# A spectral-mixing and gated-convolution kernel: one table load at the head, batch 1's folds one a step, exponents behind copies

## The chip, the cores and the metric

One Trainium2 chip; the program runs on 1 of its cores. A core has TensorE (PE, matrix products into PSUM), VectorE (DVE), ScalarE (ACT), GpSimd (POOL) and SyncE (SP, which here only starts DMAs). Each engine works through its own list of instructions in order and waits for the others by semaphores. The metric is the device time of one execution in microseconds; lower is better. Of the kernel before there are 3 runs.

## The reference

The input x has 8 batches of 3136 rows and 256 columns. The first half is the real part of a two-dimensional Fourier transform, the second a gated convolution:

```python
X = np.fft.fft(x, axis=1)
x = np.fft.fft(X, axis=2).real.astype(np.float32)
h = np.maximum(x @ w_in, 0.0)                 # 256 -> 1024
for k in range(3):                            # hp: h padded by one row on each side
    conv_out += conv_w[k] * hp[:, k:k + S, :]
gate = 1.0 / (1.0 + np.exp(-conv_out))
out = (h * gate) @ w_out                      # 1024 -> 256
```

The weights come as 64-bit floats and are narrowed to 32 bits on the chip.

## The kernel before

The transform along the rows is done as products with small tables of cosines and sines, after the input has been *folded*: rows that share a cosine or a sine up to sign are added and subtracted first. The transform along the columns is multiplied into w_in once, which gives G. So batch b needs a fold (`fold_ops`, VectorE), eight *units* of products against the tables (`units`, PE, each with a copy on ScalarE and an ending `fin` on VectorE), which give the tiles pt and qt, and then the main loop.

**The main loop** has 256 steps, one for each batch (8), chunk of rows (4) and group of 128 hidden columns (8): 32 steps a batch (`per`). Step t issues, engine by engine, work for several stages at once. On PE: `products` of step t+1 (pb from qt, then pa from pt; pb has one buffer, pa two), then `mm2` of step t-5, the block po<-wout,g of six tiles and 12 matmul records. On ScalarE: the sigmoid of step t-4 (L826), then whatever is put down under "first", `copies` of step t+1 (pb into nb, L788), what is put down under "act", the `seed` of step t+2 (L767, which writes pa before PE adds to it), the first tap (L802); and, where a chunk ends (steps 12, 20, 28 and so on), the copies of the output (L859) ahead of its stores. On VectorE: `combine` of step t (L796), what is put down under "dve", the last tap of step t-3 (L811), the gate of step t-4 (L835). On GpSimd: its share of the gate (L834), in a batch's first chunk the clearing of two columns of the next h (`row_of`, L773), the middle tap as an adding DMA (L806), what is put down under "pool", and the gathers under "load". The output of the gate of one step is the left operand of PE's block in the next.

**What is put down where** is written out in the program: a table `side` with a step and a place for each piece (`at`). The pieces that matter here:
- `shared`: in steps 0, 2, 4, 6, 8 and 10 a part of a weight is narrowed. Its first part, `power`, stands under "first": a shift on VectorE (L619) and the exponent on ScalarE (L621, a Relu activation). The second, `product`, under "dve": L633, L634, L627, L637. L627 needs the exponent.
- `Feature`: a small transform for one column; tables on ScalarE in steps 11 to 13 (L520 to L533), two products on PE in steps 14 and 16 with VectorE's L544 in step 15, and the same again in steps 31 to 34.
- The folds of batch b stand in the steps of a list `cs`, 16 operations, eight for each half of the rows: 0 pair(0) (L157), 1 pair(2) (L157, L160), 2 both(6) (L168), 3 feats(1) (L194, L195), 4 both(4) (L168), 5 turned (L228), 6 evens (L172, L173), 7 feats(0) (L194, L195), and 8 to 15 the same for the second half. `turned` multiplies by a factor and adds a copy scaled on ScalarE, `scaled` (rt<-w, L222), which for b over 0 stands under "act" in the step of operation 5 (and 13), the same step as `turned`. `scaled` reads what feats(1) and GpSimd's `single(1)` (L179, L181) write.
- For batch 1 `cs` is written out. For the others the steps go evenly from `ends[b-1]` to `ends[b]`, past steps already taken. In the step after a half's last operation the load of xh for the next batch begins: one DMA on SP, then four gathers on GpSimd (L132), one a step (for the second half three small DMAs on SP come between). Batch 2's folds stand in steps 23 to 42, with the gathers of batch 3's first half in steps 35 to 38.
- The units of batch b stand from `ends[b]` on (batch 1: two steps before it), under "pe" behind the block; copy and ending come in the step after the last part. For batch 1: one unit a step in steps 21 to 28, endings in 22 to 29. psd, the bank they use, has one buffer. Batch 1's tiles pt and qt are first read by the products issued in step 31.

ScalarE loads its function table where a function first needs one that is not in it: at the head before the copy of the taps (L698), and once more before the first sigmoid, in step 4.

Of the kernel before, what the change touches and what calls it, by code (L numbers as in the profile page):

```python
# [9 lines left out]
F32 = mybir.dt.float32  # L10
I32 = mybir.dt.int32
U32 = mybir.dt.uint32
AF = mybir.ActivationFunctionType
# [24 lines left out]
def kernel(  # L38
# [11 lines left out]
    B, S, D = x.shape  # L50
    F = moe_w_in.shape[1]
    P = 128
# [16 lines left out]
    const = ctx.enter_context(tc.tile_pool(name="const", bufs=1))  # L69
# [20 lines left out]
    act = nc.scalar.activation  # L90
# [51 lines left out]
    def fold_ops(b):  # L142

        def half(h):
            k = slice(0, NP if h == 0 else KR)
            qs = slice(2 * h, 2 * h + 2)

            def t():
                return xh[b, h]

            def pair(m):
                def f():
                    a, r = t()[k, m:m + 2], t()[k, 7 - m:5 - m:-1, ::-1, :]
                    vt(a[:, :, :, 1:D], a[:, :, :, 1:D], r[:, :, :, D - 1:0:-1], op=ALU.add)  # L157
                    if m == 2:
                        a, r = t()[k, 0:4], t()[k, 7:3:-1, ::-1, :]
                        vt(a[:, :, :, 0], a[:, :, :, 0], r[:, :, :, 0], op=ALU.add)  # L160
                return f

            def flat(i, j):
                return t()[k, i:j].rearrange("p s q d -> p (s q d)")

            def both(to, op):
                def f():
                    vt(flat(to, to + 2), flat(0, 2), flat(2, 4), op=op)  # L168
                return f

            def evens():
                vt(flat(0, 1), flat(4, 5), flat(5, 6), op=ALU.add)  # L172
                vt(flat(1, 2), flat(4, 5), flat(5, 6), op=ALU.subtract)  # L173

            def single(odd):

                def f():
                    w, s = wt[b][odd], 6 * odd
                    nc.gpsimd.tensor_copy(w[k, 0:2, qs, 0], t()[k, s:s + 2, :, 0])  # L179
                    if b:  # L180
                        nc.gpsimd.memset(w[k, 2:4, qs, P - 1:P], 0.0)  # L181
                return f

            def feats(odd):
                def f():
                    if h == 0 and odd:
                        wt[b] = [wp.tile([P, 4, HQ, P], F32, name="w", tag="w%d" % i) for i in range(2)]
                        if b == 0:
                            ea[b] = ep.tile([P, 2, HQ], F32, name="ea", tag="ea")
                            nc.gpsimd.memset(wt[b][0][0:KR, 2:4, :, P - 1:P], 0.0)  # L190
                    w, s = wt[b][odd], 6 * odd
                    v = t()[k, s:s + 2]
                    lo, hi = v[:, :, :, 1:P], v[:, :, :, D - 1:P:-1]
                    vt(w[k, 0:2, qs, 1:P], lo, hi, op=ALU.add)  # L194
                    vt(w[k, 2:4, qs, 0:P - 1], lo, hi, op=ALU.subtract)  # L195
                    if b:
                        return
                    single(odd)()
                    if odd:
                        gt(w[k, 2:4, qs, P - 1], t()[k, 7:5:-1, :, P], sg[k], op=ALU.mult)  # L200
                    else:
                        nc.gpsimd.tensor_copy(ea[b][k, :, qs], v[:, :, :, P])
                return f

            def sides():
                w = wt[b][1][0:NP, :, 2 * h]
                return w[:, 0:4:2], w[:, 1:4:2]

            made = []

            def scaled():
                if b == 0:
                    a, c = sides()
                    for i, (v, k) in enumerate(((a, 0), (c, 2), (a, 1), (c, 0))):
                        if i % 2 == 0:
                            parted[h, i // 2] = hp.tile([P, HW], F32, name="h", tag="h")[:, 0:4 * P].rearrange(
                                "p (a s d) -> p a s d", a=2, s=2)
                        act(parted[h, i // 2][0:NP, i % 2], v, AF.Copy, scale=turn[0:NP, k, h:h + 1])
                    return
                made.append(rp.tile([P, 2, 2, P], F32, name="rt", tag="rt"))  # L220
                for i, v in enumerate(sides()):
                    act(made[0][0:NP, i], v, AF.Copy, scale=turn[0:NP, 1, h:h + 1])  # L222

            def turned():
                if b == 0:
                    return
                for i, v in enumerate(sides()):
                    stt(out=v, in0=v, scalar=turn[0:NP, 0, h:h + 1], in1=made[0][0:NP, 1 - i],  # L228
                        op0=ALU.mult, op1=ALU.add if i else ALU.subtract)

            ops = [pair(0), pair(2), both(6, ALU.subtract), feats(1), both(4, ALU.add), turned, evens, feats(0)]
            return ops, {3: single(1), 7: single(0)}, {5: scaled}

        parts = [half(h) for h in range(2)]
        n = len(parts[0][0])
        return (parts[0][0] + parts[1][0],
                *[{n * h + j: f for h in range(2) for j, f in parts[h][i].items()} for i in (1, 2)])
# [363 lines left out]

    low = const.tile([P, 1], F32, name="low")
    nc.gpsimd.memset(low, -896.0 * 2 ** 23)

    def narrow(dst, raw, room=None):

# [106 lines left out]
    for f in load_ops(0, 1, nc.sync, nc.scalar, True):  # L713
        f()

    w_cv.narrow(0, 1)
    w_in[0].narrow(0, 2)
    taps()
# [192 lines left out]
    n = chunks[0].k1  # L911
# [31 lines left out]

    ends = [9, 23, per + 12] + [per * (b - 1) - 3 + max(11 - 4 * (b - 2), 0) for b in range(3, B)]
    def free(cycle):

        while cycle in taken:
            cycle += 1  # L950
        taken.add(cycle)
        return cycle
# [12 lines left out]

    for b in range(1, B):
        begin, us, *_ = units(b)
        us = us[0:4] + us[5:]

        c0 = ends[b] - 2 * (b == 1)  # L970
        n = per * b - 3 - c0
        at(max(c0, per * (b - 1) + 1), "pe", begin)
        cs = [c0 + i * n // len(us) for i in range(len(us) + 1)]
        for i, u in enumerate(us):
            k = cs[i + 1] - cs[i]
            for j in range(k):
                at(cs[i] + j, "pe", lambda u=u, j=j, k=k: u.matmuls(j, k))
            at(cs[i + 1], "act", u.copy)
            at(cs[i + 1], "dve", u.fin)
            if b > 1:  # L980
                taken.add(cs[i + 1])
        at(cs[-1] - 2, "load", lambda b=b: spread(b, range(len(chunks) - 1)))
        at(per * b + 1, "load", lambda b=b: spread(b, [len(chunks) - 1]))
    for b in range(1, B):
        ops, singles, pres = fold_ops(b)
        c0, n = ends[b - 1], ends[b] - ends[b - 1]
        if b == 1:

            cs = [9, 11, 11, 12, 12, 13, 14, 14, 16, 17, 17, 18, 19, 20, 21, 22]
            assert len(cs) == len(ops) and cs[-1] <= ends[1] and not taken & set(cs)  # L990
        else:
            cs = [free(c0 + j * n // len(ops)) for j in range(len(ops))]
            assert cs[-1] < ends[b]
        if b + 1 < B:
            for h in range(2):
                for j, fn in enumerate(load_ops(b + 1, h, nc.sync)):
                    at(cs[len(ops) // 2 * (h + 1) - 1] + 1 + j, "load", fn)
        for j, fn in enumerate(ops):
            at(cs[j], "dve", fn)
        for j, fn in singles.items():  # L1000
            at(cs[j], "pool", fn)
        for j, fn in pres.items():
            at(cs[j], "act", fn)
# [11 lines left out]
    for t in range(n + LAG):  # L1015
        def run(where):
            for fn in side.get((t, where), []):
                fn()
        if 0 <= t - 4 < n:
            sigmoid(steps[t - 4])  # L1020
        run("first")
        if t + 1 < n:
            products(steps[t + 1])
            copies(steps[t + 1])
        run("act")
        if t >= LAG:
            keep(steps[t - LAG])
        if t < n:
            combine(steps[t])
        if t + 2 < n:  # L1030
            seed(steps[t + 2])
        if t < n:
            first_tap(steps[t])

        run("dve")
        if 0 <= t - 3 < n:
            last_tap(steps[t - 3])
        if 0 <= t - 4 < n:
            gate(steps[t - 4])
        if t + 1 < n:  # L1040
            row_of(steps[t + 1])
        if t < n:
            middle(steps[t])
        run("pool")
        run("load")
        if t >= LAG:
            mm2(steps[t - LAG])
        run("pe")
# [66 lines left out]
```

## Time and profile before

| | |
|---|---|
| median of 3 runs | 1187.11 us (1185.74 to 1187.33) |
| the profiled execution | 1188.7 us, its span 1186.9 us |
| mean granted clock of TensorE | 0.994 |
| ScalarE's busy time | 945.9 us |
| GpSimd's busy time | 594.2 us |
| moved by DMA | 168.15 MB, mean 142 GB/s |

The profile is that of one execution, with times from the start of its span. Rows of a timeline give start, length, engine, source line, operation, output<-inputs and the number of records that were merged (x12); in brackets the idle time of the engine just before and what ended it. Rows of the waits give the waiter, whom it waited for, the sum in microseconds, how often, and the longest. Consecutive instructions of VectorE and ScalarE overlap by about 0.09 us in these rows, so a length is best taken from start to start. Ends of matmuls are modelled: a block's 2.75 or 2.86 us reaches a little into the products behind it.

### The profile page before, as it was taken

To read this page: it belongs to the slowest core of one execution; us is meant where nothing else is said; L and a number is where in the kernel's file an instruction comes from. 1 tells how busy PE (TensorE), PEld (TensorE's weight loads), DVE (VectorE), ACT (ScalarE), POOL (GpSimd) and SP (SyncE) were. 2 spreads that over 40 slices of the span, in tenths; PEclk is the share of its full clock that TensorE was granted. 3 is DMA by queue.
4 is the path that set the end of the run, shared out by engine and by line. 5 is a ranking of instruction groups with operands and counts; after the bars stand their busy time and mean duration, and the time that the engine had idled before them with its cause. 6 is when DMAs were issued, how large, how long until landed. Compare 5 with 4: busy or idle time off the path is not lost.

```text
span 1186.9 us, 16040 instructions
## 1 busy us (share of the span) xinstructions
PE 1144.0 (96%) x4818; PEld 890.8 (75%) x4818; DVE 963.0 (81%) x1448; ACT 945.9 (80%) x1939; POOL 594.2 (50%) x734
## 2 busy tenths in 40 slices
PE   4988999999999999999999999999999999999998
PEld 2755777777777787777777777777778777777777
DVE  7589988887888888988885887889788677788885
ACT  2488778787887888888887888888787788898884
POOL 5244745655374454556455464654444444444443
PEclk9899999999999999999999999999999999999999
DMA  8666696785677676867675576756565556666664
GB/s 206 191 99 145 152 166 147 156 174 119 136 170 160 129 157 143 169 134 170 143 162 131 94 175 143 170 128 130 117 125 117 115 122 139 131 134 124 129 119 98
DMA packets 107586, 168.15 MB, mean 142 GB/s; under 512 B 32657, under 2 KB 62627, under 8 KB 107501
## 3 DMA queue, kind: packets, MB, share of 16 engines
q0 software_dynamic: 41984, 115.83, 50.9%
q1 hardware_dynamic: 64345, 50.89, 15.1%
q8 instruction: 38, 0.62, 0.2%
q10 hardware_dynamic: 1172, 0.43, 0.2%
q14 instruction: 47, 0.39, 0.1%
HBM read 38.40 MB, written 25.74 MB: 54 GB/s over the span
## 4 chain that ended last, share of the span: by engine, by line
PE 70%; ACT 7%; DVE 6%; issue 3%; DMA 2%; POOL 2%; SPq 0%; ACTq 0%; DVEq 0%; POOLq 0%
PE po L93 44%; PE pb L93 11%; PE pa L93 10%; PE pd L93 5%; DVE g L811 2%; ACT g L826 2%; ACT nb L788 2%; ACT os L859 1%; DMA out_dram<-os 1%; POOL g L834 1%; DVE h L796 1%; DMA eb<-ed 1%; POOL xh L132 1%; ACT pa L767 1%; DMA xh<-in_x_dram 1%
## 5 line engine op out<-in xcount | busy, mean ns | idle before, releaser
L93 PE MATMUL po<-wout,g 128*128 128x256 f32 x3072 | 708.5, 380 | 10.3 <-DVE g L835 10.0
L93 PEld LDWEIGHTS po<-wout,g 128*128 128x128 f32 x3072 | 581.6, 190 | 157.8 <-DVE g L835 27.1
L806 POOL DMA_DIRECT2D g<-h x256 | 227.7, 889 | 481.5 <-ACT g L802 266.1
L826 ACT ACTIVATE g<-g,cw 128x385 f32<-128x385 f32 (+2 forms) x512 | 291.5, 621 | 77.7 <-DVE g L811 75.2
L834 POOL TENSOR_TENSOR g<-g,h 128x385 f32<-128x385 f32 (+1 forms) x256 | 287.6, 1124 | 56.9 <-ACT g L826 55.4
L788 ACT ACTIVATE nb<-pb 128x386 f32<-128x386 f32 (+3 forms) x512 | 226.1, 495 | 102.8 <-PE pb L93 101.0
L811 DVE SCALAR_TENSOR_TENSOR g<-h,cw,g 128x770 f32<-128x770 f32 (+1 forms) x256 | 288.1, 1125 | 0.0
L796 DVE CUSTOM_DVE_ANT_0 h<-pa,nb 128x386 f32<-128x386 f32 (+3 forms) x512 | 264.6, 557 | 28.4 <-POOL h L773 19.5
L802 ACT ACTIVATE g<-h,cw 128x770 f32<-128x770 f32 (+1 forms) x256 | 243.6, 952 | 0.0
L93 PE MATMUL pb<-qt,G 127*128 127x387 f32 (+2 forms) x512 | 214.5, 500 | 5.7 <-ACT nb L788 4.8
L93 PE MATMUL pa<-pt,G 128*128 128x387 f32 (+2 forms) x512 | 212.8, 496 | 0.5 <-ACT pa L767 0.4
L835 DVE TENSOR_TENSOR g<-g,h 128x385 f32<-128x385 f32 (+1 forms) x256 | 188.0, 734 | 25.3 <-ACT g L826 25.0
L767 ACT ACTIVATE pa<-eb,ge 128x387 f32<-128x387 f32 (+2 forms) x256 | 154.7, 604 | 3.2 <-DVE h L796 2.8
L93 PEld LDWEIGHTS pa<-pt,G 128*128 128x128 f32 x512 | 97.0, 190 | 75.0 <-issue 16.9
L93 PE MATMUL pd<-tab,w 98*128 98x197 f32 (+2 forms) x448 | 98.3, 318 | 3.1 <-DVE as L412 2.8
L132 POOL DMA_INDIRECT xh<-in_x_dram,idx x64 | 91.8, 1434 | 18.6 <-issue 11.5
L93 PEld LDWEIGHTS pb<-qt,G 127*128 127x128 f32 x512 | 90.8, 190 | 12.8 <-ACT nb L788 6.3
L93 PEld LDWEIGHTS pd<-tab,w 98*128 98x128 f32 (+1 forms) x448 | 81.9, 191 | 13.1 <-ACT pa L767 4.2
L859 ACT COPY os<-po 128x256 f32<-128x256 f32 x196 | 57.8, 390 | 14.5 <-DMA out_dram<-os 7.9
L157 DVE TENSOR_TENSOR xh<-xh 98x1020 f32<-98x1020 f32 (+1 forms) x32 | 47.8, 1497 | 0.0
L168 DVE TENSOR_TENSOR xh<-xh 98x1024 f32<-98x1024 f32 (+1 forms) x32 | 44.2, 1382 | 0.1
L194 DVE TENSOR_TENSOR w<-xh 98x508 f32<-98x508 f32 (+1 forms) x32 | 33.5, 1047 | 0.2
(140 smaller groups left out, 411.3 us busy)
## 6 DMA issues: line engine op xcount, KB each, us to landing
g<-h POOLq DMA_DIRECT2D x192, 385.0 KB, 4.0
g<-h POOLq DMA_DIRECT2D x64, 416.0 KB, 4.2
out_dram<-os SPq DMA_DIRECT2D x192, 128.0 KB
xh<-in_x_dram SPq DMA_DIRECT2D x16, 784.0 KB
eb<-ed SPq DMA_DIRECT2D x16, 193.5 KB
raw<-in_moe_w_in_dram SPq DMA_DIRECT2D x4, 512.0 KB
raw<-in_moe_w_out_dram SPq DMA_DIRECT2D x1, 2048.0 KB
eb<-ed SPq DMA_DIRECT2D x8, 209.0 KB
```

Source lines behind the costliest of these rows:

```text
L93: nc.tensor.matmul(o, l, r, start=start, stop=stop, skip_group_check=True)
L132: nc.gpsimd.indirect_dma_start(out=xh[b, h][0:NP, 7 - m].rearrange("p q d -> p (q d)"), out_offset=None, in_=bass.AP(tensor=x.tensor, offs ...
L767: act(pa[s][:, 0:n], eb[b, c], AF.Copy, scale=ge[:, f:f + 1])
L788: act(nb[s][:, i, cols], p[:, cols], AF.Copy, scale=-1.0 if i else 1.0)
L796: nc.vector._custom_dve(TENSOR_ADD_SAT, out=to, in0=a[:, cols], in1=c[:, i, cols], s0=BIG, s1=0.0)
L802: act(gs[s], hs[s][:, 0:n], AF.Copy, scale=cw[:, 0, s[2]:s[2] + 1])
L806: nc.gpsimd.dma_start(out=gs[s], in_=hs[s][:, 1:1 + n], accum_op=ALU.add)
L811: stt(out=g, in0=h[:, k:k + n], scalar=cw[:, k, f:f + 1], in1=g, op0=ALU.mult, op1=ALU.add)
L826: act(gs[s][:, c], gs[s][:, c], AF.Sigmoid, scale=cw[:, 1, s[2]:s[2] + 1])
L834: gt(g[:, p], g[:, p], h[:, p], op=ALU.mult)
L835: vt(g[:, v], g[:, v], h[:, v], op=ALU.mult)
L859: nc.scalar.copy(out=osb[:, j % 2], in_=pt[:, j % 2])
```

## The change

Six edits:
1. `scaled` hangs on operation 4 (and 12) in place of 5 (and 13), for batches 1 to 7; before the loop, in batch 0, it is issued with operation 4 as well.
2. A tiny sigmoid on a new tile first_use is issued at the head, ahead of the narrowing of the taps. The program then holds one table load, at the place of the first.
3. In each step `products` and `copies` come before what stands under "first", so that ScalarE's exponents (L621) come behind the copies.
4. Batch 1's folds: the list of steps is new, one operation a step but for steps 16 (two) and 10 and 15 (none), and ends in step 25, not 22. The half's `scaled` are in steps 14 and 22, its `turned` in 16 and 23.
5. Batch 1's units run in steps 22 to 29, not 21 to 28, in another order: all four odd ones first. The endings come in steps 23 to 30.
6. Batch 2's folds begin in step 28 and stand one a step to step 44 (step 32 is taken); the gathers of batch 3's first half come in steps 38 to 41. `ends` of batches 2 and 3 are 45 and 70, not 44 and 68; from batch 4 on they are as before.

```diff
-            return ops, {3: single(1), 7: single(0)}, {5: scaled}
+            return ops, {3: single(1), 7: single(0)}, {4: scaled}
...
+    first_use = const.tile([P, 1], F32, name="first_use")
...
+    act(first_use, low, AF.Sigmoid)
     w_cv.narrow(0, 1)
...
-    ends = [9, 23, per + 12] + [per * (b - 1) - 3 + max(11 - 4 * (b - 2), 0) for b in range(3, B)]
+    ends = [9, 25, per + 13, 2 * per + 6][0:B] + [per * (b - 1) - 3 + max(11 - 4 * (b - 2), 0) for b in range(4, B)]
...
-        us = us[0:4] + us[5:]
-
-        c0 = ends[b] - 2 * (b == 1)
-        n = per * b - 3 - c0
+        us = us[0:2] + us[5:7] + us[2:4] + us[7:] if b == 1 else us[0:4] + us[5:]
+
+        c0 = ends[b] - 3 * (b == 1)
+        n = per * b - (2 if b == 1 else 3) - c0
...
-            cs = [9, 11, 11, 12, 12, 13, 14, 14, 16, 17, 17, 18, 19, 20, 21, 22]
+            cs = [9, 11, 12, 13, 14, 16, *range(16, 26)]
...
+            if b == 2:
+                c0, n = c0 + 3, n - 3
...
-        run("first")
         if t + 1 < n:
             products(steps[t + 1])
             copies(steps[t + 1])
+        run("first")
         run("act")
```

## The prediction

> **What bounds the kernel now.** I read the page first: TensorE (PE) is busy nearly throughout, so only microseconds in which PE stands still can be won. Then the table of who PE waits for, asked for 90 to 151 us, then PE's timeline.
>
> ```profile
> span 1186.9 us, 16040 instructions
> PE 1144.0 (96%) x4818; PEld 890.8 (75%) x4818; DVE 963.0 (81%) x1448; ACT 945.9 (80%) x1939; POOL 594.2 (50%) x734
> ...
> PE po L93 <- DVE g L835: 6.8, 9, 1.7
> ...
> 73.42 4.07 PE L93 MATMUL po<-wout,g 128*128 128x256 f32 x12 [0.30 <-DVE g L835]
> ...
> 100.91 2.86 PE L93 MATMUL po<-wout,g 128*128 128x256 f32 x12 [0.62 <-DVE g L835]
> ...
> 120.06 0.78 PE L93 MATMUL pd<-ft 56*56 56x112 f32 x6
> ...
> 129.37 1.33 PE L93 MATMUL pd<-ft 56*29 56x168 f32 x8
> ...
> 150.10 2.86 PE L93 MATMUL po<-wout,g 128*128 128x256 f32 x12 [1.36 <-DVE g L835]
> ...
> 215.10 2.75 PE L93 MATMUL po<-wout,g 128*128 128x256 f32 x12
> 217.69 0.81 PE L93 MATMUL pb<-qt,G 127*128 127x386 f32 x2
> 218.34 0.81 PE L93 MATMUL pa<-pt,G 128*128 128x386 f32 x2
> 218.99 2.75 PE L93 MATMUL po<-wout,g 128*128 128x256 f32 x12
> ```
>
> PE is idle for 1186.9 - 1144.0 = 42.9 us. A step of the main loop ends, on PE, with one block po<-wout,g; the block at 73.42 is that of step 5, and counted on from there the one at 100.91 is that of step 11 and the one at 150.10 that of step 21. Where PE is not kept waiting a step takes 218.99 - 215.10 = 3.89, say 3.9 us: by starts 2.6 for the block and 0.65 for each of the products pb and pa. Steps 11 to 20 hold two extra pieces, of 0.78 and 1.33. PE's own need there is 10 x 3.9 + 2.1 = 41.1 us; they took 150.10 - 100.91 = 49.2. **So 8.1 us are lost there, and every marked wait in that stretch is for VectorE's gate (L835).** This is where the change puts its hand; from step 21 PE is gapless for a long time.
>
> **The change, part by part.**
>
> *Fold of batch 1 spread out.* Before, steps 11 to 20 hold fold operations 1 to 13 (counted from 0); after, by the new list of steps, 1 to 10. The three that leave are the second half's feats(1) (L194, L195), both(4) (L168) and turned (L228), and with `scaled` now tied to operation 4 the turn has its copy a step or more ahead, so its waits go too.
>
> ```profile
> 114.94 0.88 DVE L228 SCALAR_TENSOR_TENSOR w<-w,turn,rt 98x256 f32<-98x256 f32 x2 [2.31 <-POOL g L834]
> ...
> 137.10 1.53 DVE L194 TENSOR_TENSOR w<-xh 99x508 f32<-99x508 f32 x1
> 138.55 0.68 DVE L195 TENSOR_TENSOR w<-xh 99x508 f32<-99x508 f32 x1
> ...
> 141.49 1.21 DVE L168 TENSOR_TENSOR xh<-xh 99x1024 f32<-99x1024 f32 x1
> ...
> 146.43 2.21 DVE L228 SCALAR_TENSOR_TENSOR w<-w,turn,rt 98x256 f32<-98x256 f32 x2 [1.40 <-ACT rt L222]
> ```
>
> Work that leaves: 1.53 + 0.68 + 1.21 + 2.21 = 5.6, less some 0.08 of overlap each (138.55 starts before 137.10 + 1.53), 5.3. Waits that go: 2.31 + 1.40 = 3.7. VectorE paced this stretch, so its 49.2 becomes 49.2 - 9.0 = 40.2, under PE's 41.1: PE becomes the bound, and up to 8.1 come back. What is late next is ScalarE in steps 12 to 14, which holds PE's product through the seed (L767) it must write:
>
> ```profile
> 105.37 1.13 ACT L826 ACTIVATE g<-g,cw 128x385 f32<-128x385 f32 x2 [0.73 <-DVE g L811]
> ...
> 109.49 1.68 ACT L859 COPY os<-po 128x256 f32<-128x256 f32 x6
> ...
> ...
> 113.95 0.90 ACT L222 ACTIVATE rt<-w,turn 98x256 f32<-98x256 f32 x2
> 114.75 0.57 ACT L767 ACTIVATE pa<-eb,ge 128x387 f32<-128x387 f32 x1
> ```
>
> From the sigmoid at 105.37 to the seed at 114.75 ScalarE works without a pause: 9.4 us, with output copies, the feature tables and the scaled copies in it. After, the copies (0.8 by starts) lie a step later: 8.6. The sigmoid's wait of 0.73 goes, so it starts near 104.6, and the seed ends near 104.6 + 8.6 + 0.57 = 113.8. PE on its own would want it for the product pa ahead of the block of step 14, at 100.91 + 3 x 3.9 - 0.65 = 112.0. So 1.7 of the 8.1 stay, and I take **-6.5** (49.2 becomes 42.7) for steps 11 to 21. The knot gives VectorE a lead: by step 21 it is 42.7 - 40.2 = 2.5 us ahead of what PE asks.
>
> *Units and turn later.* The same eight units run one step later on PE, odd ones first: no work more or less, so 0 on PE; but VectorE's steps 23 to 25 now get the turn, evens and feats(0) of batch 1 beside the units' own endings, where before it had batch 2's first three folds. The cover is thin:
>
> ```profile
> 165.26 0.55 DVE L835 TENSOR_TENSOR g<-g,h 128x385 f32<-128x385 f32 x1
> ...
> 165.86 2.86 PE L93 MATMUL po<-wout,g 128*128 128x256 f32 x12
> ```
>
> The gate ends at 165.81 and PE's block follows at 165.86. Between nothing and the 1.3 by which a slow turn exceeds a plain one (2.21 and 0.88 above), I take **+0.3**, nearer to nothing, since the folds that leave these steps are as long as those that come. The last unit ends in step 30 and its first reader is step 31's product, a step later: 0. If that cover went, each us by which the ending is late would be PE's. The spread of eb issues one step later on SP's queue and is read two steps on: 0. Stores and loads of xh keep their order on SP but for neighbours.
>
> *Scaled copies ahead, batch 2 to 7; batch 2's folds one a step from 28.* The turn's waits on its copy are the fourth largest of VectorE's, but PE pays for one alone:
>
> ```profile
> DVE w L228 <- ACT rt L222: 21.3, 13, 3.8
> ...
> DVE h L796 <- POOL h L773: 4.6, 3, 1.9
> ...
> 211.03 0.55 DVE L835 TENSOR_TENSOR g<-g,h 128x384 f32<-128x384 f32 x1
> ...
> 241.00 1.17 DVE L228 SCALAR_TENSOR_TENSOR w<-w,turn,rt 98x256 f32<-98x256 f32 x2 [1.74 <-ACT rt L222]
> ...
> 243.03 0.55 DVE L835 TENSOR_TENSOR g<-g,h 128x385 f32<-128x385 f32 x1
> ...
> 243.63 2.86 PE L93 MATMUL po<-wout,g 128*128 128x256 f32 x12 [0.99 <-DVE g L835]
> ```
>
> That 1.74 on VectorE became 0.99 on PE at step 41: **-1.0**. The other twelve waits stand where VectorE has time. Against it, batch 2's sixteen folds now fill steps 28 to 44 instead of 23 to 42. From the gate at 211.03 (step 33) to that at 243.03 (step 40) VectorE took 4.57 a step against PE's 3.9, eating the 3.5 us by which the gate ending at 211.58 led the block at 215.10. 4.6 of these 32.0 were waits for GpSimd's memset (the h L773 row, asked for 203 to 245), which stood behind the gathers of xh for batch 3 in steps 35 to 38; these now come in steps 38 to 41, when only one memset is left; 1.74 was the copy. Without them 25.7 / 7 = 3.7 a step: it fits, barely. Between 0 and the 5.9 of the fourth rival, **+0.7**.
>
> *The table load and the exponents (L621).* This is the step that looks surest and, I think, gives nothing.
>
> ```profile
> 53.02 0.72 ACT L621 ACTIVATE win<-win,low 128x512 int32<-128x512 int32 x1
> 53.72 0.87 ACT L788 ACTIVATE nb<-pb 128x385 f32<-128x385 f32 x2
> ...
> 67.30 0.16 ACT L750 COPY ge<-po 128x2 f32<-128x2 f32 x1
> 67.48 1.28 ACT L826 ACT_TABLE_LOAD   x1
> 68.77 1.12 ACT L826 ACTIVATE g<-g,cw 128x385 f32<-128x385 f32 x2
> 69.80 0.70 ACT L621 ACTIVATE wout<-wout,low 128x512 int32<-128x512 int32 x1
> 70.42 0.84 ACT L788 ACTIVATE nb<-pb 128x385 f32<-128x385 f32 x2
> ...
> 70.54 0.69 DVE L627 SCALAR_TENSOR_TENSOR wout<-raw,wout 128x512 int32<-128x512 int32 x1 [1.85 <-ACT wout L621]
> ...
> 56.52 0.92 PE L93 MATMUL pb<-qt,G 127*128 127x386 f32 x2 [0.46 <-ACT G L740]
> ```
>
> In step 4 VectorE waits at 70.54 for the exponent. The load's 1.28 goes. But the exponent now also stands behind the two copies, 0.84 less 0.09 of overlap, so VectorE gains 1.28 - 0.75 = 0.5 there. And in step 0 the exponent at 53.02 ran while ScalarE waited for PE's product; behind the copies, which cannot start before, its 0.6 (53.72 on from 53.02, less overlap) comes on top, and PE's next product, which waits for ScalarE's G copies (56.52), is 0.6 later, and so is all up to step 4. 0.5 - 0.6 = **0.0**, between -0.6 and +0.6. In later steps the exponent has VectorE's other work before it. The first_use activation is a tiny one behind a load that is there already (the first load moves nowhere): 0.2 at most, under ScalarE's wait for the input.
>
> The Trainium skill, "ScalarE: Activation LUTs", section "What ACT_TABLE_LOAD costs", puts a switch at 1283 ns plus about 1380 ns of drain. By it the head would gain 1.4 us more; the trace agrees on 1.28 and shows no drain: the copy ends at 67.46, the load starts at 67.48 and the sigmoid at 68.77, so I leave it out. By the page the time would be 1179.2, inside the forecast's own case.
>
> Sum: 0.0 - 6.5 + 0.3 - 1.0 + 0.7 = **-6.5 us**. The profiled execution took 1188.7 with a span of 1186.9 (1.8 around it), so it would become 1182.2; it stood 1.6 above the median of the three runs shown, 1187.11, from which I forecast **1180.6**.
>
> **Rivals.**
> 1. *More than forecast.* SP's load of xh for batch 4 moves from step 68 to 69, behind the eight stores of step 68. PE's stalls behind such stores are
>
> ```profile
> 372.40 0.92 PE L93 MATMUL pb<-qt,G 127*128 127x386 f32 x2 [1.48 <-ACT nb L788]
> ...
> 652.38 0.44 PE L93 MATMUL pd<-tab,w 99*128 99x99 f32 x2 [2.52 <-DVE as L412]
> ```
>
> If both go: -1.5 - 2.5, 1176.6. Against it: the second has the same loads around it as before. 12%.
>
> 2. *The port takes half.* One fold in every step meets GpSimd's work in every step. The turn took 2.21 at 146.43 against 0.88 at 114.94. If three folds of the stretch each grow by that 1.3, VectorE needs 40.2 + 3.9 = 44.1 for steps 11 to 20, 3.0 over PE's need; if that adds to ScalarE's knot, with 0.5 more in steps 23 to 25, it is -3.0, 1184.1. The Trainium skill, "SBUF — State Buffer", section "Who interferes with whom", says that a VectorE instruction with two SBUF inputs and a GpSimd one that reads SBUF block each other outright; the two durations of the turn fit it. 17%.
>
> 3. *The change doesn't do what it says: VectorE stays the bound in steps 28 to 44*, at the 4.57 a step measured above. For 14 steps of one fold: 14 x 0.67 - 3.5 = 5.9 lost in place of my 0.7: -1.3, 1185.8, which is no change. 10%.
>
> 4. *Slower.* The same place with a mean step over 4.66: there 14 x 0.76 - 3.5 = 7.2 eats all of the rest (-6.5 + 0.3 - 1.0). At 4.9, as when both the waits on GpSimd and contended folds stay, 10.5 are lost: +3.3, 1190.4. For it: the folds are denser than ever. Against it: the two named causes of the 4.57 move away. 11%.
>
> **How the numbers follow.** The forecast's own case has 50%, within 2.5 us. The range reaches from just under rival 1 to the near side of rival 3: 1175.8 to 1185.6, leaving out some 2 in 10. A run of this kernel tells about 0.2%, 2.4 us, from no change. Faster by more (under 1184.7): nearly all of the forecast and rival 1, most of 2, a little of 3: 0.78. Same 0.11, slower 0.11.
>
> **What would show it.** Right: one ACT_TABLE_LOAD, near 10 us; PE's block of step 11 still near 100.9, of step 21 near 143.6 instead of 150.10; one gap of about 1.7 before step 14, before pa and not before po; no wait of L228 for rt. Wrong: gaps before po in steps 23 to 26 or 36 to 45 (rivals 3 and 4), the head's blocks 0.6 or more earlier (my cost of the exponents), or pair and feats over 2.5 us (rival 2).

## The result, and the profile after

| | before | after |
|---|---|---|
| median, shortest and longest | 1186.48 us (1185.74 to 1187.33, 5 runs) | 1181.0 us (1180.23 to 1182.65, 5 runs) |
| ratio of the times, 95% interval | | 0.9961, 0.9944 to 0.9978 |
| the profiled execution, its span | 1188.7 us, 1186.9 us | 1182.34 us, 1180.6 us |

The change makes the kernel 0.39% faster, 5.5 us; forecast were 1180.6 us and -6.5. From the first part of the page after:

```profile
span 1180.6 us, 16071 instructions
PE 1142.3 (97%) x4818; PEld 889.1 (75%) x4818; DVE 970.7 (82%) x1448; ACT 943.5 (80%) x1939; POOL 611.2 (52%) x734
```

PE's records are as many as before and it stands still for 1180.6 - 1142.3 = 38.3 us, 4.6 less. The other 1.7 of the 6.3 that the span lost are rows that count as busy; so idle time alone is not the whole account, and I cut the span instead. PE's timeline is read at the starts of the blocks po<-wout,g of a few steps; the first mark is the product pa that step 0 issues (53.52 before, 50.29 after). Every kernel below is cut at the same marks:

| us, from one profile each | first mark | to step 5 | 5 to 11 | 11 to 21 | 21 to 30 | 30 to 64 | 64 to 96 | 96 to 133 | 133 to 160 | 160 to end | span |
|---|---|---|---|---|---|---|---|---|---|---|---|
| before | 53.52 | 19.90 | 27.49 | 49.19 | 46.30 | 149.20 | 140.30 | 161.20 | 119.19 | 420.61 | 1186.9 |
| **after** | 50.29 | 19.82 | 28.49 | 43.18 | 47.43 | 149.99 | 138.22 | 161.20 | 121.20 | 420.78 | 1180.6 |
| *difference* | -3.23 | -0.08 | +1.00 | -6.01 | +1.13 | +0.79 | -2.08 | 0 | +2.01 | +0.17 | -6.30 |
| *forecast* | 0 | 0.0 | 0 | -6.5 | +0.3 | -0.3 | 0 | 0 | 0 | 0 | -6.5 |
| e11_again (after, unaltered) | 50.56 | 19.83 | 27.47 | 43.18 | 47.43 | 149.98 | 138.21 | 161.20 | 119.76 | 420.68 | 1178.3 |
| e1_table | 51.66 | 18.61 | 27.47 | 49.20 | 46.31 | 149.21 | 140.35 | 161.20 | 121.94 | 420.65 | 1186.6 |
| e2_exp_ahead | 50.36 | 18.61 | 27.44 | 43.19 | 47.43 | 149.97 | 138.19 | 161.22 | 119.65 | 420.64 | 1176.7 |
| e3_folds | 50.33 | 19.88 | 27.47 | 43.52 | 49.11 | 150.28 | 140.42 | 161.20 | 118.39 | 420.60 | 1181.2 |
| e4_scaled | 52.00 | 19.82 | 28.48 | 43.53 | 47.26 | 151.99 | 138.22 | 161.20 | 119.68 | 420.70 | 1182.9 |
| e5_no_late2 | 50.27 | 19.83 | 28.49 | 43.19 | 49.29 | 149.89 | 139.16 | 161.20 | 119.73 | 420.65 | 1181.7 |
| e6_tables | 50.85 | 19.83 | 28.42 | 42.13 | 47.55 | 149.97 | 138.21 | 161.20 | 119.81 | 420.63 | 1178.6 |
| e7_gathers | 52.02 | 19.82 | 27.47 | 43.19 | 45.98 | 150.37 | 138.20 | 161.21 | 119.74 | 420.70 | 1178.7 |
| e9_store_later | 50.37 | 19.83 | 28.46 | 43.18 | 47.43 | 149.97 | 138.18 | 161.20 | 114.86 | 419.32 | 1172.8 |
| e10_three | 50.36 | 18.60 | 27.49 | 43.18 | 45.97 | 150.41 | 138.20 | 161.21 | 114.85 | 419.33 | 1169.6 |

Read the columns downwards first. Most repeat within 0.1 us wherever the code of the stretch is the same. Three do not: the first mark (50.3 to 53.5), 5 to 11 (27.5 or 28.5) and 133 to 160 (118.4 to 121.9 among the kernels that are alike there). The row e11_again is the kernel after, run again: its span is 2.3 shorter: 1.02 + 1.44 shorter in the last two of the three, 0.27 longer in the first. So the -3.23 and the +2.01 of the difference row are no work of the change (the +1.00 is taken up with e2_exp_ahead); without these two columns the profiles differ by -6.30 + 3.23 - 2.01 = -5.1, and with e11_again in place of after by -6.2. The times say -5.5 and, in e11's own comparison, -6.0.

**The clock makes the difference in two of the three.** PE's timeline and a row of the windows view (busy time by engine, then the granted clock) of the kernel after:

```profile
80.30 4.53 PE L93 MATMUL po<-wout,g 128*128 128x256 f32 x12 [1.98 <-DVE g L837]
```
```profile
80.00:85.00 5.00, 4.70 (x13) 3.81 (x14) 5.00 (x9) 4.04 (x8) 2.55 (x3) 0.66 0.46 84
```

and the same of e11_again:

```profile
80.58 2.86 PE L93 MATMUL po<-wout,g 128*128 128x256 f32 x12 [1.97 <-DVE g L837]
```
```profile
80.00:85.00 5.00, 4.42 (x18) 3.52 (x19) 5.00 (x10) 4.92 (x11) 2.27 (x3) 1.00 0.43 79
```

The same block after nearly the same wait (1.98 and 1.97) took 4.53 at a clock of 0.66 in one run and 2.86 at 1.00 in the other. The kernel before had such a block too, at 73.42 (4.07 long, step 5), where the next wait swallowed it: its 5 to 11 is 27.49. The first mark moves with the same thing: between 30 and 35 us, in the head, PE had 0.66 in the profile before (the first row below) and 1.00 in the one after (the second), and before had 0.66 between 45 and 50 as well. Of the others, e1, e4 and e7, with marks of 51.66 to 52.02, show 0.71 to 0.79 between 45 and 50; those at 50.3 to 50.9 show 1.00 from 30 to 50. The third column, 133 to 160, is taken up with e9_store_later.

```profile
30.00:35.00 5.00, 5.00 (x20) 5.00 (x21) 0.00 (x0) 1.00 (x2) 0.00 (x0) 0.66 0.62 206
```
```profile
30.00:35.00 5.00, 5.00 (x29) 5.00 (x30) 0.00 (x0) 1.33 (x3) 0.00 (x0) 1.00 0.51 189
```

### The profile page after: what moved, and what is told of

It reads as the page before. It is cut to its first block, busy times and chain, and to the rows that moved or that the text cites. A ratio compares the mean times of both kernels' runs of the same rounds, so it can differ in the third digit from the quotient of the medians.

```text
span 1180.6 us, 16071 instructions
## 1 busy us (share of the span) xinstructions
PE 1142.3 (97%) x4818; PEld 889.1 (75%) x4818; DVE 970.7 (82%) x1448; ACT 943.5 (80%) x1939; POOL 611.2 (52%) x734
## 4 chain that ended last, share of the span: by engine, by line
PE 77%; ACT 5%; DVE 3%; issue 1%; DMA 1%; POOL 0%; ACTq 0%; DVEq 0%; SPq 0%
PE po L93 48%; PE pb L93 12%; PE pa L93 11%; PE pd L93 6%; ACT nb L790 1%; ACT g L828 1%; DVE g L813 1%; ACT os L861 1%; DMA out_dram<-os 1%; ACT pa L769 0%; ACT g L804 0%; DVE g L837 0%; DVE h L798 0%; DVE w L228 0%; DVE pt L418 0%
## 5 line engine op out<-in xcount | busy, mean ns | idle before, releaser
L836 POOL TENSOR_TENSOR g<-g,h 128x385 f32<-128x385 f32 (+1 forms) x256 | 305.6, 1194 | 55.9 <-ACT g L828 54.2
L813 DVE SCALAR_TENSOR_TENSOR g<-h,cw,g 128x770 f32<-128x770 f32 (+1 forms) x256 | 284.1, 1110 | 0.0
L168 DVE TENSOR_TENSOR xh<-xh 98x1024 f32<-98x1024 f32 (+1 forms) x32 | 46.7, 1460 | 0.1
L157 DVE TENSOR_TENSOR xh<-xh 98x1020 f32<-98x1020 f32 (+1 forms) x32 | 44.7, 1402 | 0.0
L385 DVE TENSOR_TENSOR as<-as,pd 128x196 f32<-128x196 f32 x14 | 5.0, 358 | 37.6 <-ACT as L381 37.6
```

What stands on the lines that cost most here:

```text
L813: stt(out=g, in0=h[:, k:k + n], scalar=cw[:, k, f:f + 1], in1=g, op0=ALU.mult, op1=ALU.add)
L836: gt(g[:, p], g[:, p], h[:, p], op=ALU.mult)
```

## The experiments

Each kernel ran beside runs of the kernel before on the same chip. Since runs of one kernel scatter by 2 to 10 us, the verdicts below stand on the columns of the table, and the ratio of the times is given beside them. None leaves out work.

### The head

**e1_table**: the kernel before with the one table load alone.

```diff
+    first_use = const.tile([P, 1], F32, name="first_use")
...
+    act(first_use, low, AF.Sigmoid)
     w_cv.narrow(0, 1)
```

> The kernel before with edit 2 alone (the tiny sigmoid at the head, one table load). Measure: from the product pa issued in step 0 (53.52 before, 50.29 after) to the block of step 5 (73.42 and 70.11): 19.90 and 19.82 us. My theory: the load of 1.28 stood in VectorE's path in step 4 and leaves it; without the exponents behind copies nothing takes it back, so this stretch becomes 19.90 - 1.28 = 18.6 and the time falls by about 1.2 us (0.1%). Rival, with a drain behind the load: 17.2 and -2.6 us. Rival, something else holds step 5: 19.9 and no change. Steps 11 to 21 stay at 49.2.

Ratio 0.9994 (0.9981 to 1.0006). The stretch to step 5: 19.90 before, 18.61 here, so **1.29**, the load's own length of 1.28 and nothing more. PE's timeline of e1_table:

```profile
51.66 0.81 PE L93 MATMUL pa<-pt,G 128*128 128x386 f32 x2
...
68.03 0.92 PE L93 MATMUL pb<-qt,G 127*128 127x386 f32 x2 [1.23 <-ACT nb L790]
...
70.27 2.86 PE L93 MATMUL po<-wout,g 128*128 128x256 f32 x12 [0.67 <-DVE g L837]
```

The wait for nb that was 2.64 at 71.31 before is 1.23. The Trainium skill, "ScalarE: Activation LUTs", section "What ACT_TABLE_LOAD costs", adds some 1380 ns of drain to a switch; by it 17.2 would stand here, and the run does not show it. The times, 1185.39 us against 1185.88, scatter too much to show the 1.2 us expected of them.

**e2_exp_ahead**: the kernel after, the exponents ahead of the copies again.

```diff
             sigmoid(steps[t - 4])
+        run("first")
         if t + 1 < n:
...
             copies(steps[t + 1])
-        run("first")
         run("act")
```

> The changed kernel without edit 3: the exponents stand ahead of the copies again. My theory: edit 3 cost what edit 2 won. In step 0 and 4 VectorE waited for the exponent 1.14 and 1.20 us, in step 8 0.94 more; so from pa of step 0 to the block of step 5 it takes 19.8 - 1.2 = 18.6 instead of 19.8, and steps 5 to 11 take about 27.5 instead of 28.5; the time is 1.2 to 2.2 us below the changed kernel's. Rival (the copies ahead were worth their place): 19.8 becomes 20.4 or more, and the time is 0.6 us or more above it.

Ratio 0.9941 (0.9920 to 0.9962). To step 5 it takes 18.61 against 19.82: edit 3 costs 1.2, all but 0.1 of what the load brings. PE and VectorE of the kernel after:

```profile
50.29 0.81 PE L93 MATMUL pa<-pt,G 128*128 128x386 f32 x2
...
52.00 0.69 DVE L628 SCALAR_TENSOR_TENSOR win<-raw,win 128x512 int32<-128x512 int32 x1 [1.14 <-ACT win L622]
...
53.89 0.92 PE L93 MATMUL pb<-qt,G 127*128 127x386 f32 x2 [1.06 <-ACT G L742]
...
67.24 0.69 DVE L628 SCALAR_TENSOR_TENSOR wout<-raw,wout 128x512 int32<-128x512 int32 x1 [1.20 <-ACT wout L622]
...
70.11 2.86 PE L93 MATMUL po<-wout,g 128*128 128x256 f32 x12 [1.46 <-DVE g L837]
```

and PE of e2_exp_ahead:

```profile
68.97 2.86 PE L93 MATMUL po<-wout,g 128*128 128x256 f32 x12 [0.67 <-DVE g L837]
```

In step 0 the product behind ScalarE's G copies waits 1.06 where it waited 0.46 before; in step 4 VectorE waits 1.20 for the exponent, and its gate holds PE's block 1.46 instead of 0.67. Edit 3 may also have a part in the slow blocks. A block of more than 4 us stands at step 5 or 7 in five of the seven profiles with edit 3 (after, e4, e5, e6, e9) and in one of the five without it (before); the waits ahead of these blocks are 1.46 and 1.98 with it, 0.67 and 1.80 here. e7_gathers and e11_again, with edit 3 and 27.47 for 5 to 11, show that it does not always bring one; that it makes one likelier is open.

### Batch 1's folds and their copies

**e3_folds**: the kernel before with batch 1's new list and unit order alone (edits 4 and 5).

```diff
-            cs = [9, 11, 11, 12, 12, 13, 14, 14, 16, 17, 17, 18, 19, 20, 21, 22]
+            cs = [9, 11, 12, 13, 14, 16, *range(16, 26)]
...
-    ends = [9, 23, per + 12] + [per * (b - 1) - 3 + max(11 - 4 * (b - 2), 0) for b in range(3, B)]
+    ends = [9, 25, per + 12] + [per * (b - 1) - 3 + max(11 - 4 * (b - 2), 0) for b in range(3, B)]
```

> The kernel before with the new steps of batch 1's folds and units alone (edits 4 and 5), the scaled copy in the same step as its turn, batch 2's folds evenly from step 25 to 44, no edit to the table, the exponents. My theory: the spreading carries the gain; from the block of step 11 to that of step 30 it took 95.5 before and 90.6 after, and should take 90.5 to 92, since the turn's waits fall where VectorE has about 2 us of lead; the time falls by 3.5 to 5 us. Rival (the gain came from the copy ahead of the turn, that is from the 3.7 us of waits that left): 94 or more, and the time falls by 1.5 us at most.

**e4_scaled**: the kernel after with the scaled copy in the turn's own step again (edit 1 undone).

```diff
-            return ops, {3: single(1), 7: single(0)}, {4: scaled}
+            return ops, {3: single(1), 7: single(0)}, {5: scaled}
```

> The changed kernel without edit 1: the scaled copy stands in the same step as its turn again, everything else as changed. My theory: steps 11 to 30 lose little (90.6 to 91.5), the turn's wait comes back on VectorE (2 us in steps 16 and 23), and about step 41 PE loses 1 us again; the time is 0.5 to 2 us above the changed kernel's. Rival (the copy ahead is what counts): 94 us or more for steps 11 to 30 and 3.5 us or more above it. In favour of a gain instead: the copy in step 22 waited 2.48 us for GpSimd and held ScalarE, and the PE gap of 0.72 in step 23 stood behind it; if that goes, 0.5 us less.

Ratios 0.9987 (0.9975 to 1.0) and 0.9982 (0.9969 to 0.9996). In 11 to 21 they take 43.52 and 43.53, after 43.18, before 49.19: spreading the folds carries 5.7 of the 6.0, the copy ahead of the turn 0.35. But e3 was expected to take 90.5 to 92 from 11 to 30 and to fall by 3.5 to 5 us; it took 92.63, and its time fell by 0.8. What the spreading wins in 11 to 21, e3 gives back behind it: 2.8 in 21 to 30 and 1.1 in 30 to 64. Edit 1 pays in this last stretch. There e4 takes 151.99 against 149.99: its largest stall,

```profile
248.80 2.86 PE L93 MATMUL po<-wout,g 128*128 128x256 f32 x12 [1.81 <-DVE g L837]
```

stands at step 43, where the kernel after has no marked wait; the largest that it has there is 0.67, at step 44 (shown below).

**e6_tables**: the kernel after with the feature tables three steps earlier, to try whether ScalarE's knot holds PE before step 14.

```diff
-        at(11 + i, "act", lambda i=i: feat.tables(i))
+        at(8 + i, "act", lambda i=i: feat.tables(i))
```

> The changed kernel with the three groups of feature tables on ScalarE in steps 8 to 10 in place of 11 to 13. My theory of the knot: ScalarE's queue in steps 11 to 13 (tables, output copies) writes the seed too late and PE loses 1.4 to 1.7 us before the block of step 14; without the tables there the stretch from the block of step 11 to that of 14 takes 11.7 to 12.2 us in place of 13.4, and steps 11 to 21 about 42.0 in place of 43.2; some of it may be lost again in steps 8 to 10 (up to 0.5). Rival (GpSimd's late half of the gate in step 13 and the slow folds hold it): 13.4 stays.

Ratio 0.9951 (0.9935 to 0.9967). First the knot in the kernel after, PE's timeline from step 11 to 14, and the block of step 21:

```profile
98.60 2.86 PE L93 MATMUL po<-wout,g 128*128 128x256 f32 x12 [0.62 <-DVE g L837]
...
108.13 1.56 PE L93 MATMUL po<-wout,g 128*128 128x256 f32 x6 [0.17 <-POOL g L836]
109.85 0.92 PE L93 MATMUL pb<-qt,G 127*128 127x387 f32 x2 [0.16 <-ACT nb L790]
111.25 0.92 PE L93 MATMUL pa<-pt,G 128*128 128x387 f32 x2 [0.48 <-ACT pa L769]
112.01 2.75 PE L93 MATMUL po<-wout,g 128*128 128x256 f32 x12
...
141.78 2.75 PE L93 MATMUL po<-wout,g 128*128 128x256 f32 x12
```

From 98.60 to 112.01 are 13.41, against 3 x 3.9 = 11.7: 1.7 lost, ahead of pb, pa and the second half of a block, with ScalarE or GpSimd's share of the gate (L836) as releaser. In e6_tables the same three steps take 11.81, so it is the tables. But PE now waits elsewhere (ScalarE's row belongs to the last of PE's):

```profile
97.03 0.92 PE L93 MATMUL pa<-pt,G 128*128 128x387 f32 x2 [0.15 <-ACT pa L769]
99.10 2.86 PE L93 MATMUL po<-wout,g 128*128 128x256 f32 x12 [1.15 <-DVE g L837]
...
114.19 0.91 ACT L222 ACTIVATE rt<-w,turn 98x256 f32<-98x256 f32 x2 [2.16 <-POOL w L181]
...
115.62 0.92 PE L93 MATMUL pa<-pt,G 128*128 128x387 f32 x2 [0.41 <-ACT pa L769]
```

Steps 8 to 11 take 14.23 against 13.28 in runs without the slow block, and 14 to 21 take 30.32 against 29.77; 1.6 gained, 1.5 given back, where up to 0.5 was expected. The first loss lies where the tables now stand; in the second the scaled copy of step 14 waits 2.16 for GpSimd's small pieces and the seed behind it is late, the chain of the next experiment. The knot is moved, not loosened.

### Steps 21 to 30, and batch 2's folds

**e7_gathers**: the kernel after with the four gathers that follow batch 1's first half on GpSimd four steps later (steps 23 to 26).

```diff
-                    at(cs[len(ops) // 2 * (h + 1) - 1] + 1 + j, "load", fn)
+                    at(cs[len(ops) // 2 * (h + 1) - 1] + 1 + j + (4 if (b, h) == (1, 0) and j else 0), "load", fn)
```

> The changed kernel with the four gathers of batch 2's first half on GpSimd in steps 23 to 26 in place of 19 to 22. My theory of the loss in steps 21 to 30 (47.4 us, 46.3 before): the gathers and GpSimd's small copies make the scaled copy of step 22 wait 2.48 us, the turn of step 23 is late and PE's unit loses 0.72 or more; without the gathers there it is 46.3 to 46.7. Rival (VectorE's own folds beside the units' endings hold it): 47.4 stays, or it grows where the gathers now stand.

Ratio 0.9936 (0.9915 to 0.9956). In the kernel after (GpSimd, then ScalarE's scaled copy, the turn, and PE's unit that reads it):

```profile
142.82 2.56 POOL L132 DMA_INDIRECT xh<-in_x_dram,idx  x1 [0.30 <-issue]
...
146.81 2.01 POOL L179 COPY w<-xh 99x4 f32<-99x4 f32 x1
...
148.89 0.91 ACT L222 ACTIVATE rt<-w,turn 98x256 f32<-98x256 f32 x2 [2.48 <-POOL w L181]
...
153.22 0.36 DVE L385 TENSOR_TENSOR as<-as,pd 128x196 f32<-128x196 f32 x1 [3.51 <-ACT as L381]
...
153.76 1.82 DVE L228 SCALAR_TENSOR_TENSOR w<-w,turn,rt 98x256 f32<-98x256 f32 x2
...
155.64 0.97 PE L93 MATMUL pd<-tab,w 98*128 98x197 f32 x4 [0.72 <-DVE w L228]
```

and in e7_gathers:

```profile
146.24 0.50 POOL L179 COPY w<-xh 99x4 f32<-99x4 f32 x1
...
147.00 0.92 ACT L222 ACTIVATE rt<-w,turn 98x256 f32<-98x256 f32 x2
...
152.40 0.36 DVE L385 TENSOR_TENSOR as<-as,pd 128x196 f32<-128x196 f32 x1 [1.38 <-ACT as L381]
...
152.95 0.87 DVE L228 SCALAR_TENSOR_TENSOR w<-w,turn,rt 98x256 f32<-98x256 f32 x2
...
154.32 1.57 PE L93 MATMUL pd<-tab,w 98*128 98x197 f32 x8
```

The whole chain is gone: a gather of 2.56 ahead of a copy of four columns, which itself takes 2.01 instead of 0.50, makes the scaled copy 2.48 late. ScalarE's copy of the unit before (L381) stands behind that, VectorE waits 3.51 for it instead of 1.38, and the turn comes behind this wait and itself takes 1.82 instead of 0.87; so the next unit is late, and PE runs it in two halves. The stretch falls from 47.43 to 45.98, 0.3 below the kernel before; 0.4 of it comes back in 30 to 64, where four small gate waits stand in place of three.

**e5_no_late2**: the kernel after with batch 2's folds in their old steps (edit 6 undone).

```diff
-    ends = [9, 25, per + 13, 2 * per + 6][0:B] + [per * (b - 1) - 3 + max(11 - 4 * (b - 2), 0) for b in range(4, B)]
+    ends = [9, 25, per + 12] + [per * (b - 1) - 3 + max(11 - 4 * (b - 2), 0) for b in range(3, B)]
...
-            if b == 2:
-                c0, n = c0 + 3, n - 3
```

> The changed kernel without edit 6: batch 2's folds evenly from step 25 to 44 as its list puts them, batch 3's and 4's as before. Two effects of edit 6 to part. In steps 21 to 30: the folds kernel, with batch 2's folds from 25, took 49.1 us there, the changed one 47.4; my theory is that the collision of batch 2's folds with batch 1's units costs 1.7, so 49.1 here; the rival, that the scaled copy in the turn's step cost it, gives 47.4. From the block of step 64 to that of 96: 140.3 before, 138.2 after; my theory is that the input load of batch 4, one step later, came behind the stores of step 68 and took 1.5 of PE's stall away; without edit 6 it is 140.3 again. Rival (batch 3's folds): about 138.

Ratio 0.9963 (0.9941 to 0.9985). In 21 to 30 it takes 49.29, and e3_folds, which also lacks edit 6, 49.11: without it batch 2's first folds meet batch 1's units, and two gate waits come that the kernel after does not have:

```profile
169.20 2.86 PE L93 MATMUL po<-wout,g 128*128 128x256 f32 x12 [0.43 <-DVE g L837]
...
175.27 2.86 PE L93 MATMUL po<-wout,g 128*128 128x256 f32 x12 [0.91 <-DVE g L837]
```

So edit 6 is worth 1.9 there. In 30 to 64 it is worth nothing: 149.89 against 149.99. The waits of the kernel after in that stretch, all that are marked on PE:

```profile
230.70 0.82 PE L93 MATMUL pa<-pt,G 128*128 128x387 f32 x2
231.69 2.86 PE L93 MATMUL po<-wout,g 128*128 128x256 f32 x12 [0.18 <-DVE g L837]
...
236.17 2.86 PE L93 MATMUL po<-wout,g 128*128 128x256 f32 x12 [0.31 <-DVE g L837]
...
247.40 0.81 PE L93 MATMUL pa<-pt,G 128*128 128x387 f32 x2
248.88 2.86 PE L93 MATMUL po<-wout,g 128*128 128x256 f32 x12 [0.67 <-DVE g L837]
251.57 0.82 PE L93 MATMUL pb<-qt,G 127*128 127x387 f32 x2
```

Here one sees what a short wait costs. Without one a block starts 0.65 after pa and lasts 2.59 to the next pb. The one marked 0.67 starts 1.48 after pa and lasts 2.69: 0.83 + 0.10 = 0.93 lost, 0.26 more than is marked (0.16 of it is the modelled end of pa, which reaches that far into the usual start of the block); the one marked 0.18 loses 0.34 + 0.1 = 0.44 in the same way, the one marked 0.31 some 0.57. The three sum to 1.9; the single wait of 0.99 before, with 0.26 on top, to 1.25. That is +0.7 of the +0.8 of the stretch.

In 64 to 96 e5 takes 139.16, e3 140.42, after 138.22. That is less of the way back than the 140.3 expected. The place is SP's queue where batch 1's last chunk ends (step 68). The kernel before, ScalarE and SP in order of time:

```profile
362.66 0.35 SPq L119 DMA_DIRECT2D xh<-in_x_dram  x1
...
365.42 6.38 SPq L861 DMA_DIRECT2D out_dram<-os  x8
...
370.20 0.37 ACT L859 COPY os<-po 128x256 f32<-128x256 f32 x1 [3.44 <-DMA out_dram<-os]
```

after:

```profile
358.73 5.31 SPq L863 DMA_DIRECT2D out_dram<-os  x8
...
361.11 0.37 ACT L861 COPY os<-po 128x256 f32<-128x256 f32 x1 [1.03 <-PE pa L93]
...
364.28 0.38 SPq L119 DMA_DIRECT2D xh<-in_x_dram  x1
```

and e5_no_late2, where the load of xh is issued ahead of the stores again:

```profile
364.90 0.37 ACT L861 COPY os<-po 128x256 f32<-128x256 f32 x1 [3.07 <-DMA out_dram<-os]
```

With 784 KB of xh ahead of them ScalarE's last copy waits for stores to land, that is for the buffer that they read: 3.44 and 3.07 with the load ahead, none for the DMA with it behind. Of the 2.1 that the stretch gained, undoing edit 6, which puts batch 3's folds back with the load, gives 0.94 back here; e3_folds, without edits 1 to 3 as well, stands where the kernel before does. Edit 2 is not the other part by itself (e1_table, 140.35), and e4_scaled and e2_exp_ahead, without edit 1 and without edit 3, keep 138.2; what softens the stall in e5 was not found.

### The stores at a batch's end

**e9_store_later**: the kernel after, with the last output copy of batches 1, 3 and 5 and its stores two steps later. It tries whether the stall in step 132, where the column 133 to 160 scatters, is this same wait for a buffer.

```diff
+                def put(i=i, pt=pt):
...
+                if i == 6 and b + 1 < B:
+                    at(per * (b + 1) - 1 + LAG + 2, "act", put)
+                else:
+                    put()
```

> The changed kernel with the copy and stores of the seventh output tile of batches 1, 3 and 5 two steps later. My theory of the stall at step 132 (3.53 us of PE, and two products at nearly half the pace behind it): four output tiles share three buffers, and ScalarE's queue stands until the first store has landed; two steps later the buffer is free, and from the block of step 133 to that of 160 it takes 116.8 or less in place of 118.4 to 121.9 in the runs so far. From 64 to 96: 138.2 or a little less. The time falls by 2 to 4 us. Rival (PE waits for something else there): 118.4 to 121.9 as it comes.

1174.61 us (1174.46 to 1176.74), ratio 0.9899 (0.9868 to 0.9930). The kernel after, ScalarE and PE:

```profile
641.73 0.37 ACT L861 COPY os<-po 128x256 f32<-128x256 f32 x1 [4.19 <-DMA out_dram<-os]
...
644.90 0.72 PE L93 MATMUL pd<-tab,w 99*128 99x99 f32 x2 [3.53 <-DVE as L412]
645.42 1.54 PE L93 MATMUL pb<-qt,G 127*128 127x386 f32 x2
```

e9_store_later (PE's row is that of the same unit):

```profile
641.21 0.37 PE L93 MATMUL pd<-tab,w 99*128 99x99 f32 x2
...
644.80 0.36 ACT L862 COPY os<-po 128x256 f32<-128x256 f32 x1
```

The last chunk of a batch with an odd number fills four output tiles, and there are three buffers (`osp`). The fourth copy stands on ScalarE until stores have landed, 4.19 here; what stands behind it on ScalarE is late, then VectorE's ending, then PE by 3.53, and after that stop two products ran at 1.5 instead of 0.8. Two steps later the buffer is free. 133 to 160 falls to 114.86, under all of those above, and 160 to the end by 1.4, together more than the 2 to 4 us expected. The scatter of the column goes with PE's stop and with the clock between 645 and 650 us behind it: 3.53 and 0.50 in the kernel after (121.20), 3.27 and 0.80 in e11_again (119.76), 2.50 and 1.00 in e3_folds (118.39). Why the stores land so late here is open: SP issued nothing for 28 us ahead of them, and at step 68 of the kernel after the same four tiles wait for no store.

**e10_three**: e2, e7 and e9 together. **e11_again**: the kernel after, unaltered, beside it.

> The changed kernel with three edits of the runs so far together: exponents ahead of the copies, batch 2's gathers in steps 23 to 26, the seventh output tile's copy two steps later. If their gains lie in different stretches and add: from pa of step 0 to the block of step 5 18.6 us (19.8 in the changed kernel), steps 21 to 30 46.0 (47.4), steps 133 to 160 114.9 (118.4 to 121.9), the rest after 160 419.3 (420.7); together some 1.2 + 1.4 + 5.1 + 1.4 = 9 us below the changed kernel, near 1172. Rival (what one gives back another stretch takes, as with the tables in steps 8 to 10): 1175 or more.

> The changed kernel once more, unaltered, on the same chip as the run beside it. It tells which stretches differ by themselves: pa of step 0 has stood at 50.3 to 53.5 us, the step from the block of 7 to that of 8 took 4.0 or 5.7, and 133 to 160 118.4 to 121.9. My theory: the 1.0 us more in steps 5 to 11 of the changed kernel (28.5, before 27.5) comes with a slow clock in step 7 (0.66 granted in 80 to 85 us) and not from the order of the exponents, so it comes or goes between runs of one kernel; all other stretches stay within 0.1 (11 to 21 43.2, 21 to 30 47.4, 30 to 64 150.0, 64 to 96 138.2). Rival (edit 3 costs it, by the wait of 0.94 in step 8): 28.5 again with a step 8 of 4.0.

e10_three: **1171.12 us** (1170.9 to 1173.2), ratio **0.9859** (0.9837 to 0.9882), faster than both kernels. e11_again: 1181.24 (1177.94 to 1184.43), ratio 0.9943 (0.9922 to 0.9965).

The three gains add: 18.60 is e2's, 45.97 e7's, 114.85 e9's column, and 5 to 11 is 27.49.

## Why the prediction was right, and where it was not

- **Head, 0.0: right, and for the reason given.** -0.08 measured. The two halves are near what I had: the load is worth 1.29 (1.28 forecast) and edit 3 costs 1.2 (0.75 in step 4 and 0.6 in step 0 forecast). No part of the drain shows.
- **Steps 11 to 21, -6.5: right in mechanism and nearly in size, -6.0.** VectorE ceased to be the bound, by the spread folds (e3). What remained was the knot on ScalarE at the step that I had named, and its 1.7 go nearly all with the tables (e6). My own figures, 113.8 - 112.0, give 1.8 for it, and 8.1 less that is 6.3, not 6.5. It is also not one gap before pa: the marked waits are 0.17 within a block, 0.16 before pb and 0.48 before pa. Of the missing 0.5, 0.4 stand in steps 14 to 21: 29.77 against 7 x 3.9 + 2.1 = 29.4, with no marked wait; they hold the two extra pieces, whose price I took from their lengths alone.
- **Steps 21 to 30, +0.3: the term was mis-sized, +1.1.** I priced the turn's longer duration and not the queue behind which its copy stands: SP's and POOL's orders were looked at for batch 2, not for batch 1, whose gathers in steps 19 to 22 stood ahead of the small copy in step 22 (e7). In the same place a gain was missed: batch 2's folds leave it (1.9, e5).
- **Steps 30 to 64, -1.0 + 0.7: wrong in sign, +0.8.** None of the turns waits for its copy any more (13 times, 21.3 us, before), and the 0.99 at step 41 is 0.31. But the step "without them ... it fits, barely" failed: VectorE was late by 0.2 to 0.7 three times, which is rival 3's mechanism at a small part of its 5.9, and each short wait costs 0.26 beyond its mark. Edit 1 is what keeps it small (e4: 2.0 more). The later folds of batch 2, on which I had put the +0.7, are not what costs it: with them back in their old steps the stretch takes as long (e5, 149.89).
- **Steps 64 to 96, 0: wrong, -2.1.** Rival 1's first half came true, the stall behind step 68's stores, and at least 0.9 of it for its reason (e5). Its second half did not, the stall in step 132 is still there, as the argument against it said.
- **Rivals 2 and 4.** VectorE's turn took 0.87 or 1.82 us and GpSimd's copy 0.50 or 2.01 (e7), which fits rival 2's mechanism but was not parted from other causes; no block of PE behind that of step 11 and up to that of step 21 waited for VectorE's gate, so no 3.0 came of it. Rival 4's place lost 1.9 in marked waits, not 7.2.

The errors of +0.5, +0.8 and +1.1 stood against one of -2.1, so that the sum of the terms, -6.5, came out at -6.1 (the difference row's other columns) outside the three columns that scatter, or at -5.1 if the +1.00 of 5 to 11 is edit 3's. That is luck: the whole is nearer than its parts deserve.

## What to carry to other kernels

When an instruction is moved behind others on its engine, ask what it did there: the exponent ran while ScalarE waited for PE anyway, and moved, it took back nearly all that the missing table load had won. When folds or loads are shifted, follow every in-order queue that they share, down to a copy of four columns behind a gather, and a last output copy behind stores that have yet to land. Where runs scatter by more than the effect, cut the span at fixed marks and compare the pieces: here most of them repeat to 0.1 us.

## What the hardware showed that was not expected

After waits of 1.5 to 2 us PE ran the next block at a granted clock of 0.66 in some runs and at 1.00 in others of the same program (4.53 and 2.86 us for one block); in 5 to 11 it costs nothing or 1.0 us, by what waits behind. A copy of 99x4 on GpSimd took 0.50 or 2.01 us. The longer one began at 146.81, while a VectorE sum of two tiles (L168) ran from 145.30 to 147.36, as "Who interferes with whom" of the Trainium skill's "SBUF — State Buffer" would have it; but in e7_gathers the start of that sum at 146.52 lies within the copy's 0.50 too, so that which overlap is dear was not settled.
